# Decode attention over a long cache: key loads a pair ahead, values of the preceding pair inside the next pair's keys

## The chip, the cores and the metric

The kernel runs on one core of a Trainium2 chip. The metric is the device time of one execution in microseconds. Before the change the median of three runs was 1266.62 us (1266.15 to 1267.58). The engines are named as in the profile: PE is TensorE (PEld its weight loads), DVE VectorE, ACT ScalarE, POOL GpSimd, SP SyncE; SP only issues DMAs here.

## The reference

One token is decoded. Its row `x` (448 numbers) gives 16 query heads of 256; each of 8 key/value heads serves two of them. Every head attends to 65536 cached keys and values. A small token MLP of the same row is mixed in by a gate.

```python
q = (x @ wq).reshape(B, Sq, Hq, Dh).transpose(0, 2, 1, 3)
scores = einsum("bhqd,bhkd->bhqk", q, k) * (Dh ** -0.5)     # k, v repeated for the two query heads
p = softmax(scores)
o = einsum("bhqk,bhkd->bhqd", p, v)
a = o.transpose(0, 2, 1, 3).reshape(B, Sq, Hq * Dh) @ wo
h = layernorm(B_x); u = gelu(einsum("bsd,sf->bdf", h, w1) + b1); b = (einsum("bdf,fs->bds", u, w2) + b2)
g = sigmoid((x * gate_w).sum(-1))
return g * a + (1 - g) * b
```

The two caches hold 8 x 65536 x 256 bfloat16 numbers each, 268 MB each, and every number is used once. All else is small.

## The kernel before

*Tiling.* A head's 65536 positions are cut into chunks of 2048 (`CH`): 128 partitions by 16 positions (`NT`). Eight chunks (`BODY`) are a "pair", 16384 positions: 8.39 MB of keys and as many of values. There are four pairs a head (`PPH`), 32 in all (`NP`). A pair's tile is 128 partitions by 128 rows (`NV`) of 256.

*Buffers.* `kring` holds one and a half pairs of keys (192 rows); even pairs lie at rows 0 to 127, odd ones at 64 to 191, and the first four chunks of either parity are taken from the middle 64 rows, so that half a pair's place is free after four chunks. `vbuf` holds one pair of values.

*TensorE, pair by pair.* `keys` (L342 to L353): 16 transposes a chunk (L334, as float32 pairs) bring the keys into PSUM (`kst`); DVE and ACT each copy two of four banks to `ktT` (L616, L751); then 32 small matmuls (`scores`, L353) make the chunk's scores. The transposes of chunk k stand before the scores of chunk k-1. `values` then begins with `maxima` (L374, L376): the pair's largest score is found by DVE, TensorE and DVE in turns (L622 to L645), ACT makes the exponentials `pT` (L738), and DVE rescales the accumulator `acc` (L637, L645). TensorE waits for that (`s_acc`, `sem_exp`), adds the denominators (L392, eight matmuls), and the values (L403, 128 matmuls). The last of them releases `sem_pv`.

*After a head.* DVE takes the sums (`take`, L650), TensorE and DVE turn them (L439, L676), and TensorE multiplies with the head's `A_wo` rows (L450). During the first 14 pairs DVE also works off one part of the MLP (`mixer`, L591 to L609) behind the maxima, and TensorE adds its result (L513).

*SP's order of issues* (L262 to L300). For each pair j: wait until four chunks of pair j-1 are transposed, load K(j); wait until values j-1 are done, load V(j). At a head's start it then waits for the preceding head's projection and loads the next `A_wo` rows. The last two pairs of keys are cut in pieces with semaphores of their own (`sem_kp`, `sem_kq`), the last pair of values in rows 0 to 95, 96 to 111, 112 to 123, 124 to 127. After these come the two pieces of the last `A_wo`.

*The last pair.* Eight matmuls without use (`spin`, L369) stand after its maxima, and before them the MLP's row is added (L386), which DVE made before the last head's loop (`s_mix`, L699 to L702). After 112 rows of values DVE takes the sums while TensorE adds the other 16 rows in the turned form (`late_values`, L424); DVE scales (L663), the last projection runs (L450), and the row goes out (L713, L758, L300).

All loops are run-time loops over registers, one for the heads and one for the pairs within, so the program's code is one pair long.

Of the kernel before, what the change touches and what calls it, by code (L numbers as in the profile page):

```python
# [12 lines left out]
def bass_gated_mix__gqa_block_cached__mixer_token_mlp__decode_kernel(  # L13
# [17 lines left out]
    H = A_k_cache.shape[1]  # L31
# [12 lines left out]
    NT = 16  # L44
# [19 lines left out]
    NFIRST = 96  # L64
    NLATE = 112
    pieces = [(NFIRST, NLATE), (NLATE, 124), (124, NV)]
# [16 lines left out]
    QV = NV // 4  # L83
# [10 lines left out]
    with ctx:  # L94
# [101 lines left out]
        sem_kp = new_sem("sem_kp")  # L196
        sem_kq = [new_sem("sem_kq%d" % i) for i in range(3)]
# [54 lines left out]
        def _(eng):  # L252
# [13 lines left out]
            for j in range(NP):  # L266
                last = j == NP - 1
                if j >= 1:
                    eng.wait_ge(sem_tr[NB - 1], BODY * (j - 1) + DC)
                if j == 0:  # L270
                    load(kring, A_k_cache, j, HV, NV, 0, sem_k)
                    load(kring, A_k_cache, j, 0, HV, 0, sem_kb)
                elif last:
                    for i, sem in enumerate([sem_k] + sem_kq):
                        load(kring, A_k_cache, j, i * QV, (i + 1) * QV, HV, sem)
                elif j == NP - 2:
                    load(kring, A_k_cache, j, HV, NV, 0, sem_k)
                    load(kring, A_k_cache, j, 0, HV, 0, sem_kp)
                else:
                    load(kring, A_k_cache, j, 0, NV, HV * (j % 2), sem_k)  # L280
# [5 lines left out]
                load(vbuf, A_v_cache, j, 0, NFIRST if last else NV, 0, sem_v)  # L286
                if last:
                    for (n0, n1), sem in zip(pieces, sem_vp):
                        load(vbuf, A_v_cache, j, n0, n1, 0, sem)
                g, m = divmod(j, PPH)  # L290
                if m == 0 and 1 <= g < H - 1:
                    eng.wait_ge(s_proj, g)
                    load_wo(g)

            eng.wait_ge(s_proj, H - 1)
# [19 lines left out]
        def _(pe):  # L315
# [3 lines left out]
            def transposes(k, c, j, u16, x2):  # L319
                if k == 0:  # L320
                    pe.wait_ge(sem_k, u16)
                if k == DC:
                    pe.wait_ge(sem_kb, 16)
                    with pe.If(j == NP - 2):
                        pe.wait_ge(sem_kp, 16)
                if k and k % (DC // 2) == 0:
                    with pe.If(j == NP - 1):
                        pe.wait_ge(sem_kq[k // (DC // 2) - 1], 16)
# [17 lines left out]
            def scores(k, c):  # L346
                par = k % 2
                for nt in range(NT):
# [10 lines left out]
            def keys(c0, *where):  # L359
                transposes(0, c0, *where)  # L360
                for k in range(1, BODY):
                    transposes(k, c0 + k, *where)
                    scores(k - 1, c0 + k - 1)
                scores(BODY - 1, c0 + BODY - 1)


            def spin(n):
                for _ in range(n):
                    pe.matmul(kst[:, NB - 1, :], ones_sq[:, :], ktT[:, KTB - 1, 0, 0:512], start=True, stop=True)  # L369
# [9 lines left out]
            def values(j, c0, u16):  # L379
                j1 = pe.snap(j + 1, min_val=1, max_val=NP)  # L380
                maxima(j1)
                with pe.If(j == NP - 1):
# [5 lines left out]
                    spin(8)  # L388
                pe.wait_ge(s_acc, j1)
                pe.wait_ge(sem_exp, j1)  # L390
                for r in range(BODY):
                    pe.matmul(acc[:, DENC:SELC], ones_sq[:, :], pT[:, r, :],  # L392
                              start=False, stop=(r == BODY - 1), skip_group_check=True)

                def some(n0, n1, last=False):
                    if last:
                        piece_wait(n0)
                    else:
                        pe.wait_ge(sem_v, u16)
                    for n in range(n0, n1):  # L400
                        r, nt = divmod(n, NT)
                        o = 32 * (n % 4)
                        ins = pe.matmul(acc[o:o + REP, 0:DH], pT[:, r, 2 * nt:2 * nt + 2], vbuf[:, n, :],  # L403
                                        start=False, stop=False, skip_group_check=True)
                    return ins

                some(0, NFIRST)
                with pe.If(j < NP - 1):
                    some(NFIRST, NV).then_inc(sem_pv, 1)
                with pe.Else():  # L410
                    some(NFIRST, NLATE, last=True).then_inc(s_early, 1)
                    tail()
# [43 lines left out]
            def tail():  # L456
# [3 lines left out]
                spin(1)  # L460
# [39 lines left out]
            x2_reg = pe.alloc_register("x2_reg")  # L500
            pe.reg_mov(x2_reg, 0)
            on = OrderedEngineSet([pe.engine])
            with nc.Fori(0, H, 1, engines=on, head_slot={pe.engine: 0}) as g:
                with nc.Fori(0, PPH, 1, engines=on, head_slot={pe.engine: 0}) as m:
                    j = pe.snap(g * PPH + m, min_val=0, max_val=NP - 1)
                    c0 = pe.snap(j * BODY, min_val=0, max_val=NC)
                    u16 = pe.snap(j * 16 + 16, min_val=16, max_val=16 * NP)
                    keys(c0, j, u16, pe.snap(x2_reg, min_val=0, max_val=NV))
                    values(j, c0, u16)
                    with pe.If(j < FT):  # L510
                        pe.wait_ge(s_pb, j + 1)
                        for q in range(NCG):
                            pe.matmul(prj[32 * q:32 * q + 1, WG:2 * WG], w2cur[:, :],  # L513
                                      gu[:, q * WG:(q + 1) * WG], start=False, stop=True, skip_group_check=True)
                    pe.reg_sub(x2_reg, NV, x2_reg)
                with pe.If(g < H - 1):
                    pe.wait_ge(s_cp, g + 1)
                    clear(acc[:, 0:NACC])
                    by_row(acc[:, SELC:NACC]).then_inc(s_sel, 1)
                    pe.wait_ge(sem_wo, pe.snap(g * 16 + 16, min_val=16, max_val=16 * H))  # L520
                    pe.wait_ge(s_oTn, g + 1)
                    project(range(2 * REP)).then_inc(s_proj, 1)

        @block.vector
        def _(vec):
# [140 lines left out]
            def finish_head(g):  # L666
                take(vec.snap(g * PPH + PPH, min_val=PPH, max_val=NP))
                vec.memset(mrun[:, :], LOW)
                vec.tensor_copy(qcur[:, :, :], qT[:, :, bass.ds(g * REP + REP, REP)])
                vec.drain()  # L670
# [4 lines left out]
                vec.wait_ge(s_sel, g + 1)  # L675
# [5 lines left out]
            vec.tensor_copy(qcur[:, :, :], qT[:, :, 0:REP])  # L681
# [106 lines left out]
```

## Time and profile before

| what | value |
|---|---|
| runs, median (lowest, highest) | 1266.62 us (1266.15, 1267.58) |
| the profiled execution | 1267.84 us, its span 1266.0 us |
| mean clock granted to TensorE | 0.852 |
| busy: PE, PEld, DVE, ACT | 976.4, 889.4, 498.6, 545.5 us |
| read from HBM | 544.22 MB, 430 GB/s over the span |
| chain that ended last, by share | DMA 66%, PE 32%, "issue" 1%, DVE 1% |
| TensorE idle at L334, for keys to land | 144.7 us, 29 times |

The span runs from the first instruction to the last of one profiled execution. "Busy" counts the time in which an engine had an instruction running. The chain is followed back from the last instruction, at each step to what released it. In its rows the three columns are the start, the duration and what ran; "issue" is time in which the engine waited for nothing that the profile shows. In a table of windows each row has the stretch, its length, busy time with the number of instructions for PE, PEld, DVE, ACT and POOL, then the clock granted to TensorE (1.00 is full speed), the share of the DMA engines' time and GB/s.

### The profile page before, as it was taken

To read this page: it belongs to the slowest core of one execution; us is meant where nothing else is said; L and a number is where in the kernel's file an instruction comes from. 1 tells how busy PE (TensorE), PEld (TensorE's weight loads), DVE (VectorE), ACT (ScalarE), POOL (GpSimd) and SP (SyncE) were. 2 spreads that over 40 slices of the span, in tenths; PEclk is the share of its full clock that TensorE was granted. 3 is DMA by queue.
4 is the path that set the end of the run, shared out by engine and by line. 5 is a ranking of instruction groups with operands and counts; after the bars stand their busy time and mean duration, and the time that the engine had idled before them with its cause. 6 is when DMAs were issued, how large, how long until landed. Compare 5 with 4: busy or idle time off the path is not lost.

```text
span 1266.0 us, 39302 instructions
## 1 busy us (share of the span) xinstructions
PE 976.4 (77%) x17210; PEld 889.4 (70%) x17210; DVE 498.6 (39%) x1125; ACT 545.5 (43%) x692; POOL 0.9 (0%) x7
## 2 busy tenths in 40 slices
PE   2877788777787777778687887778877787886888
PEld 2766678766687767677676876668777677776787
DVE  2434345344454444444233433324333334342443
ACT  0544345443355443454334543335443345433554
POOL 0000000000000000000000000000000000000000
PEclk9888788888888878888788898888877788887899
DMA  9999999999999999999999999999999999999998
GB/s 417 430 430 424 431 433 433 433 431 433 433 437 433 433 433 433 437 433 433 431 435 437 431 433 433 433 437 433 429 437 431 435 433 433 435 433 429 431 424 355
DMA packets 12056, 544.39 MB, mean 430 GB/s; under 512 B 1417, under 2 KB 1676, under 8 KB 2956
## 3 DMA queue, kind: packets, MB, share of 16 engines
q1 hardware_dynamic: 11954, 544.22, 99.6%
q8 instruction: 8, 0.13, 0.0%
q14 instruction: 4, 0.03, 0.0%
q10 hardware_dynamic: 90, 0.01, 0.0%
HBM read 544.22 MB, written 0.00 MB: 430 GB/s over the span
## 4 chain that ended last, share of the span: by engine, by line
DMA 66%; PE 32%; issue 1%; DVE 1%; SPq 0%; DVEq 0%
DMA kring<-in_A_k_cache_dram 66%; PE kst L334 25%; PE sps L353 5%; PE acc L403 1%; PE kst L369 0%; PE sps L376 0%; DVE mcol L622 0%; DVE acc L645 0%; PE acc L392 0%; PE sps L374 0%; DVE mrow L627 0%; PE sps L424 0%; DVE mdiag L629 0%; PE sps L431 0%; DVE mcol L625 0%
## 5 line engine op out<-in xcount | busy, mean ns | idle before, releaser
L751 ACT ACTIVATE ktT<-kst 128x1024 bf16<-128x1024 bf16 x512 | 499.7, 1023 | 555.7 <-PE kst L334 555.3
L334 PE MATMUL kst<-ident,kring 128*128 128x128 f32 x4096 | 555.4, 296 | 164.8 <-DMA kring<-in_A_k_cache_dram 144.7
L334 PEld LDWEIGHTS kst<-ident,kring 128*128 128x128 f32 x4096 | 504.5, 154 | 177.5 <-issue 174.6
L616 DVE COPY ktT<-kst 128x1024 bf16<-128x1024 bf16 x512 | 354.1, 692 | 606.9 <-PE kst L334 583.3
L353 PEld LDWEIGHTS sps<-qcur,ktT 128*128 128x128 bf16 x8192 | 237.8, 96 | 5.1 <-issue 2.6
L353 PE MATMUL sps<-qcur,ktT 128*128 128x2 bf16 x8192 | 236.7, 163 | 2.1 <-issue 2.1
L403 PE MATMUL acc<-vbuf,pT 128*2 128x256 bf16 x4080 | 177.2, 356 | 0.0
L403 PEld LDWEIGHTS acc<-vbuf,pT 128*2 128x2 bf16 x4080 | 116.5, 108 | 52.5
L392 PE MATMUL acc<-pT,ones_sq 128*128 128x32 bf16 x256 | 12.7, 190 | 51.0 <-DVE acc L645 51.0
L734 ACT ACTIVATE fade<-mdif 128x2 f32<-128x2 f32 x32 | 6.6, 205 | 95.5 <-DVE mdif L633 95.5
L392 PEld LDWEIGHTS acc<-pT,ones_sq 128*128 128x128 bf16 x256 | 9.5, 106 | 54.1 <-DVE acc L645 53.6
L376 PEld LDWEIGHTS sps<-mdiag,mones 2*128 2x128 f32 x64 | 13.7, 264 | 27.8 <-DVE mdiag L629 27.8
L376 PE MATMUL sps<-mdiag,mones 2*128 2x2 f32 x64 | 16.4, 324 | 21.2 <-DVE mdiag L629 21.2
L622 DVE TENSOR_REDUCE mcol<-sps 128x2 f32<-128x256 f32 x32 | 13.6, 424 | 44.4 <-PE sps L353 44.4
L738 ACT ACTIVATE pT<-sps,mneg 128x64 f32 x128 | 30.5, 336 | 0.0
L755 ACT ACTIVATE z_b<-z_b 128x448 bf16<-128x448 bf16 x14 | 8.1, 579 | 47.9 <-DVE z_b L603 47.9
L374 PE MATMUL sps<-ident,mcol 128*2 128x128 f32 x32 | 9.1, 283 | 24.1 <-DVE mcol L625 24.1
L374 PEld LDWEIGHTS sps<-ident,mcol 128*2 128x2 f32 x32 | 2.6, 80 | 26.9 <-DVE mcol L625 26.9
L645 DVE TENSOR_SCALAR acc<-acc,fader 128x256 f32<-128x256 f32 x32 | 15.8, 492 | 2.5
L650 DVE COPY accs<-acc 128x288 f32<-128x288 f32 x8 | 3.7, 458 | 32.8 <-PE acc L403 32.8
L627 DVE TENSOR_REDUCE mrow<-sps 2x1 f32<-2x128 f32 x32 | 8.9, 278 | 12.0 <-PE sps L374 12.0
L632 DVE TENSOR_SCALAR mneg<-sps 128x2 f32<-128x2 f32 x32 | 5.1, 159 | 19.4 <-PE sps L376 19.4
(108 smaller groups left out, 169.1 us busy)
## 6 DMA issues: line engine op xcount, KB each, us to landing
kring<-in_A_k_cache_dram SPq DMA_DIRECT2D x4, 4096.0 KB, 24.4
kring<-in_A_k_cache_dram SPq DMA_DIRECT2D x4, 2048.0 KB, 26.3
vbuf<-in_A_v_cache_dram SPq DMA_DIRECT2D x1, 6144.0 KB, 27.0
wo_sb<-in_A_wo_dram SPq DMA_DIRECT2D x7, 448.0 KB, 22.8
vbuf<-in_A_wq_dram SPq DMA_DIRECT2D x1, 3072.0 KB, 11.1
vbuf<-in_A_v_cache_dram SPq DMA_DIRECT2D x1, 1024.0 KB, 29.2
vbuf<-in_A_v_cache_dram SPq DMA_DIRECT2D x1, 768.0 KB, 30.6
vbuf<-in_A_wq_dram SPq DMA_DIRECT2D x1, 512.0 KB, 12.7
```

Source lines behind the costliest of these rows:

```text
L334: ins = pe.transpose(kst[:, b, i * P:(i + 1) * P], kring_f[:, at + NT * (k % DC) + 4 * b + i, :], ident[:, :])
L353: ins = pe.matmul(sps[:, 0, 2 * (NT * k + nt):2 * (NT * k + nt) + 2], ktT[:, par, b, ntl * DH + dj:(ntl + 1) * DH:2], qcur[:, dj, :], star ...
L374: pe.transpose(mxT, mcol[:, :], ident[:, :]).then_inc(s_mT, 1)
L376: pe.matmul(mxB, mones[:, :], mdiag[:, :], start=True, stop=True).then_inc(s_mB, 1)
L392: pe.matmul(acc[:, DENC:SELC], ones_sq[:, :], pT[:, r, :], start=False, stop=(r == BODY - 1), skip_group_check=True)
L403: ins = pe.matmul(acc[o:o + REP, 0:DH], pT[:, r, 2 * nt:2 * nt + 2], vbuf[:, n, :], start=False, stop=False, skip_group_check=True)
L616: vec.tensor_copy(ktT[:, k % KTB, b, :], kst_b[:, b, :]).then_inc(sem_ev[b], 1)
L622: vec.tensor_reduce(out=mcol[:, :], in_=scores_all.rearrange("p (n hh) -> p hh n", hh=REP), axis=AX.X, op=ALU.max)
L627: vec.tensor_reduce(out=mrow[:, :], in_=mxT, axis=AX.X, op=ALU.max)
L645: vec.tensor_scalar(acc[:, 0:DENC], acc[:, 0:DENC], fader[:, :], None, op0=ALU.mult).then_inc(s_acc, 1)
L738: ins = act.activation(pT[:, bass.ds(p0, DC), hh:2 * NT:REP], scores_all.rearrange("p (a r n hh) -> p a hh r n", a=2, r=DC, hh=REP)[:, hal ...
L751: act.activation(ktT[:, k % KTB, b, :], kst_b[:, b, :], AF.Copy).then_inc(sem_ev[b], 1)
```

## The change

SP issues the keys a pair further ahead from the third pair on (`LEAD = 2`): after K0, V0, K1, V1 follow K2 and K3 (each in two halves), then V2, K4, V3, K5 and so on, up to K31, V30, and V31 in five pieces. Rows 0 to 47 of V31 go into `kring`, whose lower part no key needs any more; they wait only for pair 30's transposes, the others for values 30.

TensorE has one loop in place of two, with three blocks that are each run or skipped by comparing registers: seven chunks of pair k's keys; the values of pair k-1, and the head's end if that pair was its last; the eighth chunk of pair k, the MLP's part and the maxima. In the first two pairs keys and values take turns as before; from then on each pass runs all three blocks. The scores of a chunk 0 wait for the exponentials of the preceding pair (`sem_exp`), since they overwrite its scores. DVE follows: the head's end stands between the copies of chunks 6 and 7 of the next head's first pair, and the queries of the next head are set with a semaphore of their own (`s_qc`). The matmuls without use are gone. DVE makes the MLP's row after the last maxima.

```diff
-    NFIRST = 96
+    LEAD = 2
     NLATE = 112
-    pieces = [(NFIRST, NLATE), (NLATE, 124), (124, NV)]
+    NRING = 48
+    pieces = [(0, NRING), (NRING, 96), (96, NLATE), (NLATE, 124), (124, NV)]
...
             for j in range(NP):
+                if j == LEAD + 1:
+                    eng.wait_ge(sem_tr[NB - 1], BODY * LEAD)
+                    load(kring, A_k_cache, j, HV, NV, HV, sem_kc[1])
                 if j >= 1:
                     eng.wait_ge(sem_tr[NB - 1], BODY * (j - 1) + DC)
...
+                if j < LEAD:
+                    load_v(j)
+                elif j > LEAD:
+                    load_v(j - 1)
+            for (n0, n1), sem in zip(pieces, sem_vp):
+                if n0 == 0:
+                    eng.wait_ge(sem_tr[NB - 1], BODY * (NP - 1))
+                elif n0 == NRING:
+                    eng.wait_ge(sem_pv, NP - 1)
+                load(kring if n1 <= NRING else vbuf, A_v_cache, NP - 1, n0, n1, 0, sem)
...
-            def scores(k, c):
+            def scores(k, c, j1):
                 par = k % 2
+                if k == 0:
+                    pe.wait_ge(sem_exp, j1)
...
+            def keys(c0, j, *where):
+                j1 = pe.snap(j + 1, min_val=1, max_val=NP)
+                transposes(0, c0, j, *where)
+                for k in range(1, BODY - 1):
+                    transposes(k, c0 + k, j, *where)
+                    scores(k - 1, c0 + k - 1, j1)
+            def last_keys(c0, x2):
+                transposes(BODY - 1, c0 + (BODY - 1), None, None, x2)
+                for k in range(BODY - 2, BODY):
+                    scores(k, c0 + k, None)
...
-                    spin(8)
...
+            with nc.Fori(0, NP + LEAD + 1, 1, engines=on, head_slot={pe.engine: 0}):
+                with pe.If(val(k_reg) < val(cap_reg)):
...
+                    keys(pe.snap(j * BODY, min_val=0, max_val=NC), j,
...
+                with pe.If(val(v_reg) < val(l_reg)):
...
+                    values(v)
...
+                    with pe.If(val(mv_reg) == PPH):
...
+                with pe.If(val(l_reg) < val(k_reg)):
...
+                    last_keys(pe.snap(l * BODY, min_val=0, max_val=NC), pe.snap(x2l_reg, min_val=0, max_val=NV))
...
+                    maxima(pe.snap(l_reg, min_val=1, max_val=NP))
...
-            with nc.Fori(0, H - 1, 1, engines=on) as g:
+            with nc.Fori(0, H, 1, engines=on) as g:
                 with nc.Fori(0, PPH, 1, engines=on) as m:
...
-                    for k in range(BODY):
+                    for k in range(BODY - 1):
                         evacuate(k, c0 + k)
+                    with vec.If(j > 0):
+                        with vec.If(m < 1):
+                            finish_head(g)
+                    evacuate(BODY - 1, c0 + (BODY - 1))
                     maxima(vec.snap(j + 1, min_val=1, max_val=NP), c0)
...
-            take(1, s_early)
+            take(NP, s_early)
```

More of the change, by code (lines that the diff above doesn't have):

```diff
@@ L264, in load, with load_v @@
                               ).then_inc(sem, 16)
[L266 to L280, printed above, removed]
+            load(kring, A_k_cache, 0, HV, NV, 0, sem_k)
+            load(kring, A_k_cache, 0, 0, HV, 0, sem_kb)
+            def load_v(j):
                 if j == 0:
@@ L285, in _ @@
                     eng.wait_ge(sem_pv, j)
[L286 to L289, printed above, removed]
+                load(vbuf, A_v_cache, j, 0, NV, 0, sem_v)
                 g, m = divmod(j, PPH)
@@ L387, in values @@
                                   skip_group_check=True)
[L388 to L409 removed]
+                    piece_wait(0)
+                    some(0, NRING, kring)
+                for n0, n1 in pieces[1:]:
+                    if n0 < NLATE:
+                        last(lambda: piece_wait(n0))
+                        ins = some(n0, n1, vbuf)
+                ins.then_inc(s_early, 1)
+                with pe.If(v < NP):
+                    some(NLATE, NV, vbuf).then_inc(sem_pv, 1)
                 with pe.Else():
[L411 removed]
                     tail()
```

152 lines of the change are left out of this document (98 added, 54 removed).

## The prediction

> **What bounds the kernel now.** I read the head of the page first, for who is busy and whether a transfer is ever missing:
>
> ```profile
> PE 976.4 (77%) x17210; PEld 889.4 (70%) x17210; DVE 498.6 (39%) x1125; ACT 545.5 (43%) x692; POOL 0.9 (0%) x7
> ...
> DMA  9999999999999999999999999999999999999998
> GB/s 417 430 430 424 431 433 433 433 431 433 433 437 433 433 433 433 437 433 433 431 435 437 431 433 433 433 437 433 429 437 431 435 433 433 435 433 429 431 424 355
> ...
> q1 hardware_dynamic: 11954, 544.22, 99.6%
> ```
>
> The DMA engines are full in every slice but the last, at one rate. Then the chain that ended last, in order of time, around the last pairs:
>
> ```profile
> 1097.88 27.32 DMA kring<-in_A_k_cache_dram
> 1125.33 5.38 PE kst L334 x32
> ...
> 1135.90 28.93 DMA kring<-in_A_k_cache_dram
> 1164.95 6.14 PE kst L334 x32
> ...
> 1185.49 1.86 PE kst L334 x16
> 1187.35 1.59 PE sps L353 x64
> 1188.97 0.42 DVE mcol L622
> ...
> 1192.84 0.40 PE acc L392 x8
> 1193.24 5.59 PE acc L403 x111
> 1198.82 0.41 issue
> ...
> 1224.86 5.14 PE acc L403 x127
> ...
> 1254.49 2.68 PE kst L369 x8
> 1257.38 3.86 PE acc L403 x101
> 1261.27 0.47 DVE accs L650
> ...
> 1262.41 0.80 PE sps L424 x32
> 1263.47 0.40 PE prj L450 x16
> ```
>
> Up to 1164.95 each pair begins when its keys land. Landings (the first L334 of a pair) are 38.70 us apart, 39.83 where an A_wo load lies between: 618.81, 657.52; 1125.33, 1164.95. A pair is 16.78 MB, so 433.5 GB/s, and one K or V load is 19.35 us of the stream. From pair 29's landing I continue the stream: before, K30 1203.65, V30 1223.0, K31 1242.35, V31 1261.7; the V31 pieces (issue from 1230.06 on, 27.0 to 30.7 us to land) come to 1257.06 up to 1262.05, and the last A_wo to about 1263. That fits a stream with no gap to within 0.4 us. TensorE ends 1261.24, beside it. So both stream and TensorE end the kernel, and all the time there is to win is what lies after 1262; a transfer issued too late is lost one for one.
>
> **The change part by part.** The profiled execution took 1267.84 us for a span of 1266.0 (1.84 around it); the median of the runs is 1266.62, so I add span differences to that median.
>
> *Bytes, rate.* The same 544.22 MB on the same queue, in another order: K(j+1) goes ahead of V(j). Cost 0, while every load is issued before the load ahead of it has drained. So I check each issue, with a step beginning at K(s)'s landing T. Four chunks of keys take 10.4 us (1125.33 to 1135.90), so K(s+1) is issued at T+10.5; V(s-1) drains until T+19.35: 8.8 us to spare. Seven chunks take 20.5 in pair 29 (1164.95 to 1185.49), of which 6.14 are the first two; these vary from 5.04 to 6.67 in the chain, so about 20.1. Values then start at T+20.2, after V(s-1) landed, take 5.6 to 6.0 (L392 0.40, L403 5.14 to 5.59), and V(s) is issued at T+26.3, with K(s+1) draining until T+38.7: 12 us to spare. Last chunk 3.45 (1185.49 to 1188.94) and maxima 2.3 end the step at T+32.5, 6 us before the next keys. A head's end adds 3.6 (652.7 to 655.9 and its gap) in a step of 39.83. The mixer (4.4 us on DVE, pairs 0 to 13) now runs ahead of the next pair's first evacuation and not beside the values: T+33 to T+38. All hidden; cover gone costs at most what exceeds 6 us, then 8.8.
>
> *What stood idle per pair.* TensorE's waits for the maxima (51.0 + 24.1 + 21.2 us at L392, L374, L376, 3 us a pair): the exponentials now have a whole seven chunks of cover. It gains nothing in a steady pair, where TensorE waits for keys anyway (144.7 us).
>
> *The two split loads at pairs 2 and 3.* K3's second half waits for all of pair 1 (about 95) and drains from 112 on; K3's first half waits for half of pair 2, which starts after values 1, about 107.3 + 9.1 = 116.4, and the queue has work until 121.9: 4 us to spare. V2 is queued right behind it on SP. Cost 0.
>
> *The last step, by the clock of before.* K31 now lands 19.35 earlier, at 1223.0; V30 at 1242.35. Then in TensorE's order, each from a row above:
> - seven chunks 0.1 + 20.1: 1243.2, 0.9 after V30, so the keys decide;
> - branches and registers 0.4 (the "issue" row), denominators 0.4, 128 values 5.2: 1249.2. The rest of V31 is issued here. V31's first 48 chunks (now into the free half of the key ring) land at 1249.6, so the queue is all but empty. The shortest whole DMA in the trace, the x row, takes 1.36 from issue to landing (0.73 to 2.09): chunks 48 to 95 land by 1249.25 + 1.36 + 7.26 = 1257.9 and not 1256.9. The gap is 1.0 us; V31's end 1262.7 to 1263.0, A_wo's 1264;
> - gap 0.4, last chunk 3.45: 1253.05;
> - maxima to denominators 3.90 (1188.94 to 1192.84): 1256.95;
> - denominators 0.4; meanwhile DVE prepares the MLP row (L699, L701, L702: 0.28 + 0.16 + 0.24, with drains 0.75), which it did ahead of the last head and now does after the last maxima; four small matmuls 0.25: 1257.8. So 0.45 is new on the path;
> - 112 values: 1262.5 (below);
> - from the last of these to the end 1261.24 to 1266.0, 4.76 in the same steps: 1267.3. V31's last piece is wanted at 1263.7 and A_wo at 1264.7, so the stream's gap is covered by 0.7 us.
>
> *The eight spin matmuls gone.* They ran inside the maxima (1254.49, 2.68 us) and kept the clock up. The windows by stretch show what the clock is worth:
>
> ```profile
> 1193.00:1199.00 6.00, 5.82 (x136) 3.82 (x133) 0.00 (x0) 0.00 (x0) 0.00 (x0) 0.64 1.01 437
> ...
> 1224.80:1230.00 5.20, 5.20 (x131) 3.49 (x128) 0.00 (x0) 0.00 (x0) 0.00 (x0) 0.69 1.02 435
> ...
> 1257.30:1261.20 3.90, 3.90 (x116) 2.72 (x112) 0.00 (x0) 0.00 (x0) 0.00 (x0) 0.82 0.93 361
> ```
>
> 128 values took 5.59 at 0.64 granted and 5.14 at 0.69; 112 took 3.86 at 0.82: duration times clock is 3.6 for 128, 3.15 for 112. Without the spin I take 0.67 for values 31, the middle of the two pairs without one: 4.7, against 3.9. The lowest grant in the trace, 0.50 (1165 to 1170, after a wait for keys), would make it 6.3, 1.6 more. [...]
>
> *Sum.* 1267.3 against 1266.0: +1.3 us, and 1266.62 + 1.3 = 1267.9. Its own profiled execution would be about 1269.1.
>
> Bounds. Lower: first two chunks 5.04 (-0.6), both groups of values at the clock of the spun ones (-0.8, -0.8) give -0.9, but A_wo at 1263 and L450 to the end, 2.53, hold it at -0.5. Upper: first chunks 6.67 (+1.0), values at 0.64 (+0.4, +0.2) or at 0.50 (+1.6), and up to six more branches on this path than before, at 0.31 to 0.42 each where the sequencer is not ahead (+2.1): +5 to +6.
>
> **Rivals.** A measurement of this kernel can tell about 0.2%, 2.5 us, from no change.
>
> 1. *The last step is longer than I add up* (slower). The place is the stretch from K31's landing to the end, which TensorE now walks alone; it decides once 1.2 us more than my sum come together from the clock (0.50 to 0.82 in the rows) and the branches. For it: the chain there has no slack left after V30, and every row of it varies by 10%. Against: TensorE's queue runs ahead of most branches, seen in values with a branch at 96 and no gap. Price: +2.6 to +6, 1269.2 to 1272.
>
> 2. *Fetching code in the first passes holds V1 up* (slower). Before, the first pass stood still with nothing to wait for 5.41 us (24.07 to 29.48), 1.78 (before the last scores) and 2.46 (before L513), later passes not; the page counts 8 instruction packets of 0.13 MB. Now the first passes jump over blocks not yet run: past the values, back, past the keys. V1 was issued at 65.42 and the stream runs dry at about 72.1 (K1's landing 73.5, less 1.4), so 6.7 to spare. Three jumps at the mean 3.2 less the 1.78 replaced: 7.9, a gap of 1.2; at 5.41 each 14.4, a gap of 7.8. Against: the fetch ahead may have loaded the blocks. Price on top of the sum: 1269.1 to 1275.7. [...]
>
> 3. *The code no longer stays loaded.* TensorE's program is some 5% longer, all inside one loop. If a pass fetched three pages at 3.2, 9.6 us against 6 free would cost 3.6 in each of 30 steps: about 1375. Nothing in the trace points at a limit just there.
>
> 4. *Faster.* The stream would have to end 2.5 us sooner; landings 38.70 or 39.83 apart all the way from pair 2 to pair 29 leave no gap to close, and the tail after A_wo gives 0.5. 1264 or less needs something the trace does not show.
>
> That the loads are not really ahead would show as an unchanged order of landings and give 1266.6, within "no change".
>
> **How the numbers follow.** No change that can be told, with 1267.9 as its time (its own range 1265.5 to 1269.1): 0.55. Rival 1: 0.22. Rival 2: 0.13. Rival 3: 0.05. Faster: 0.05. Slower is 0.22 + 0.13 + 0.05 = 0.40. The range of 1265.5 to 1272.0 leaves out rival 3, most of faster, and the upper half of rival 2, together 0.16.
>
> **What would show it.** Landings of keys still 38.70 apart; TensorE's waits at L392, L374, L376 unchanged for the maxima (they still run alone) but the one for the exponentials gone; K31's transposes at about 1223 and values 30 ending about 1249; the last group of 112 values at about 1258 and taking 4.5 to 5; the stream's DMA share low for about 1 us near 1250. I am wrong if key landings drift apart in the middle, if V1 is issued after 72, or if the last V piece, and not TensorE, is what ends the chain.

## The result: slower by half a per cent

| | before | after |
|---|---|---|
| runs, median (lowest, highest) | 1266.58 us (1266.07, 1267.58) | 1273.26 us (1272.60, 1274.62) |
| the profiled execution, its span | 1267.84, 1266.0 us | 1273.45, 1271.7 us |
| clock granted to TensorE | 0.852 | 0.840 |

The ratio is 1.0053, with a 95% interval of 1.0040 to 1.0066. That is slower by 6.7 us where 1.3 us was forecast, and above the range given.

The head of the page after the change, with the same rows as those shown of before:

```profile
PE 941.5 (74%) x17201; PEld 884.7 (70%) x17201; DVE 498.2 (39%) x1125; ACT 545.8 (43%) x692; POOL 0.9 (0%) x7
...
DMA  9999899999999999999999999999999999999998
GB/s 415 430 399 428 377 429 429 443 429 429 429 429 443 429 429 451 439 410 449 441 429 429 443 429 429 429 443 429 429 429 429 443 429 429 429 451 439 429 429 344
...
q1 hardware_dynamic: 11810, 544.22, 99.2%
q8 instruction: 9, 0.15, 0.0%
```

The bytes are the same. One digit of the DMA row has changed from 9 to 8: the fifth slice (127 to 159 us), at 377 GB/s where before had 431. The third slice (64 to 95 us) has 399 where before had 430. A slice is 31.8 us, so these rows say that the stream broke off early in the run, once above all.

The chain, in order of time, for the last step:

```profile
1200.58 27.11 DMA kring<-in_A_k_cache_dram
...
1227.82 5.88 PE kst L344 x32
...
1248.38 3.59 PE acc L400 x128
1251.97 0.69 issue
1252.66 1.96 PE kst L344 x16
1254.62 1.59 PE sps L365 x64
...
1261.06 5.82 PE acc L400 x112
```

K31's transposes begin at 1227.82 where 1223.1 was forecast: 4.7 us late. From there to the end of the span it takes 43.9 us; the forecast had 44.2, and before, which ended at 1266.0, would have had 42.9 from 1223.1. So 4.7 us came from late keys and 1.0 from the last step: 5.7, the difference of the two spans. The medians differ by 6.7, because the profiled execution of before, 1267.84 us, took longer than each of its six timed runs, while that of after lies near its median.

*Where the keys became late.* In the same view a key load lands where its DMA row ends. Each pair's keys should land 19.35 us, one load of the stream, earlier than before. Pair 6's landed at 268.12 before, so the forecast for them is 248.77; after had them at 253.95, 5.2 late. From there to K31's landing at 1227.69 the distance is 973.74 us, and in the forecast 1222.88 - 248.77 = 974.11 (1222.88 is the forecast's 1223.0, counted to the end of the DMA row and not to the first transpose). In between the landings stand 38.70 or 39.83 apart as before (566.02, 604.72, 643.43, 682.13, 721.96). All that K31 is late by was lost in the first 254 us, and only 0.4 us of it came back.

The windows by stretch show the loss. First before, then after, the same three stretches (columns as in the prediction, the last three being granted clock, DMA share, GB/s):

```profile
70.00:75.00 5.00, 1.38 (x7) 1.39 (x8) 0.17 (x1) 0.00 (x0) 0.00 (x0) 0.50 1.14 488
...
150.00:155.00 5.00, 4.00 (x19) 4.01 (x20) 1.38 (x2) 1.32 (x2) 0.00 (x0) 0.50 0.97 419
155.00:160.00 5.00, 5.00 (x77) 4.98 (x76) 2.65 (x4) 3.62 (x5) 0.00 (x0) 0.88 0.97 419
```

```profile
70.00:75.00 5.00, 0.91 (x14) 0.41 (x7) 0.00 (x0) 0.00 (x0) 0.00 (x0) 0.50 0.94 357
...
150.00:155.00 5.00, 4.54 (x51) 4.40 (x51) 1.38 (x2) 2.29 (x3) 0.00 (x0) 0.63 0.63 210
155.00:160.00 5.00, 5.00 (x97) 4.98 (x95) 2.77 (x4) 3.38 (x4) 0.00 (x0) 1.00 0.57 249
```

Between 150 and 160 us the difference is 5 x (419 - 210) + 5 x (419 - 249) = 1895 GB/s x us, which is 4.4 us at 433.5 GB/s. Between 70 and 75 it is 1.5, of which a third comes back at once. Summed over all windows of 5 us up to a point, after is 1.0 to 2.3 us behind from 75 to 150, and 6.5 behind at 160; this sum, which goes by bytes, stands at 7.2 at 280 and at 5.3 at 300, near the 5.2 by which the landings are late.

Why it broke off shows in SP's own timeline of after, its DMA issues (V1, K2 and K3 in halves together, V2, K4):

```profile
70.64 0.33 SPq L264 DMA_DIRECT2D vbuf<-in_A_v_cache_dram  x1
85.49 33.48 SPq L264 DMA_DIRECT2D kring<-in_A_k_cache_dram  x4
119.02 0.43 SPq L264 DMA_DIRECT2D vbuf<-in_A_v_cache_dram  x1
153.57 0.33 SPq L264 DMA_DIRECT2D kring<-in_A_k_cache_dram  x1
```

and in TensorE's timeline around K4's issue (idle time before a group, and what ended it, in brackets):

```profile
134.65 3.67 PE L344 MATMUL kst<-ident,kring 128*128 128x128 f32 x16 [0.68 <-issue]
141.17 3.67 PE L344 MATMUL kst<-ident,kring 128*128 128x128 f32 x16 [2.85 <-DVE ktT L674]
...
145.53 3.65 PE L344 MATMUL kst<-ident,kring 128*128 128x128 f32 x16
```

K4 waits for four chunks of pair 3. These took from 134.65 to 153.5, 18.9 us, where the forecast had 10.5. The second chunk waits 2.85 us for a DVE copy, and every chunk up to the fourth takes 3.65 us or more for its 16 transposes, not 1.95: in windows of 1 us the granted clock is 0.50 from 134 to 153. DVE's timeline says what it did meanwhile:

```profile
135.74 0.34 DVE L649 TENSOR_SCALAR wtmp<-hbT,params 128x448 bf16<-128x448 bf16 x1 [0.18 <-issue]
...
139.71 0.39 DVE L667 TENSOR_TENSOR gu<-wtmp,z_b 128x448 bf16<-128x448 bf16 x1
140.42 1.29 DVE L674 COPY ktT<-kst 128x1024 bf16<-128x1024 bf16 x2 [0.32 <-issue]
```

That is pair 2's part of the MLP, 135.7 to 140.1, behind the maxima of pair 2 and ahead of the first copies of pair 3's keys. When K4 was issued the queue was empty; a finer window has not one byte between 149.80 and 153.50 (V2's landing itself is put at 152.1):

```profile
149.80:153.50 3.70, 3.70 (x30) 3.64 (x27) 1.38 (x2) 1.47 (x2) 0.00 (x0) 0.50 0.00 0
```

*The first passes.* TensorE's timeline has three long waits for nothing that the profile shows, each where code is reached that has not run yet or a pass begins anew: ahead of pair 0's last chunk, which is reached by a jump over the values; within values 0, after 80 of its matmuls, where kernel.py has no branch (its branches stand after rows 48, 96 and 112); and ahead of pair 1's keys, after the jump back (these had landed at 72.46, so they account for less than half of the last wait):

```profile
51.43 3.54 PE L344 MATMUL kst<-ident,kring 128*128 128x128 f32 x16 [8.06 <-issue]
...
68.09 2.52 PE L400 MATMUL acc<-vbuf,pT 128*2 128x256 bf16 x48 [2.90 <-issue]
74.70 5.59 PE L344 MATMUL kst<-ident,kring 128*128 128x128 f32 x32 [4.09 <-issue]
```

V1 is issued at 70.64 (before 65.42).

### The profile page after: what moved, and what is told of

Same layout as the page of the kernel before. It is cut to its first block, busy times and chain, and to the rows that moved or that the text cites. A ratio compares the mean times of both kernels' runs of the same rounds, so it can differ in the third digit from the quotient of the medians.

```text
span 1271.7 us, 40084 instructions
## 1 busy us (share of the span) xinstructions
PE 941.5 (74%) x17201; PEld 884.7 (70%) x17201; DVE 498.2 (39%) x1125; ACT 545.8 (43%) x692; POOL 0.9 (0%) x7
## 4 chain that ended last, share of the span: by engine, by line
DMA 61%; PE 35%; DVE 2%; issue 2%; DVEq 0%; ACT 0%; SPq 0%
DMA kring<-in_A_k_cache_dram 61%; PE kst L344 27%; PE sps L365 6%; PE acc L400 2%; PE sps L388 0%; DVE mcol L680 0%; ACT z_b L816 0%; PE acc L458 0%; PE sps L386 0%; PE acc L393 0%; DVE ktT L674 0%; DVE mrow L685 0%; DVE z_b L655 0%; DVE wtmp L653 0%; DVE z_b L659 0%
## 5 line engine op out<-in xcount | busy, mean ns | idle before, releaser
L344 PE MATMUL kst<-ident,kring 128*128 128x128 f32 x4096 | 574.9, 303 | 251.6 <-DMA kring<-in_A_k_cache_dram 198.0
L344 PEld LDWEIGHTS kst<-ident,kring 128*128 128x128 f32 x4096 | 522.2, 158 | 266.6 <-issue 259.7
L400 PE MATMUL acc<-vbuf,pT 128*2 128x256 bf16 x4032 | 121.6, 281 | 2.9 <-issue 2.9
L400 PEld LDWEIGHTS acc<-vbuf,pT 128*2 128x2 bf16 x4032 | 94.2, 86 | 21.9 <-issue 3.4
L393 PEld LDWEIGHTS acc<-pT,ones_sq 128*128 128x128 bf16 x256 | 8.6, 97 | 12.4 <-issue 7.0
```

Source lines behind the costliest of these rows:

```text
L344: ins = pe.transpose(kst[:, b, i * P:(i + 1) * P], kring_f[:, at + NT * (k % DC) + 4 * b + i, :], ident[:, :])
L393: pe.matmul(acc[:, DENC:SELC], ones_sq[:, :], pT[:, r, :], start=False, stop=(r == BODY - 1), skip_group_check=True)
```

## The experiments

Three theories. *M*: pair 2's part of the MLP holds pair 3's first copy, so K4 is issued after the stream ran dry; priced at 3 to 4 us. *Code*: fetches of code in the first passes hold V1, K2 and K3 up; 1 to 2 us. *Last step*: the step from K31 on is longer by about 1 us, in part because the MLP's row is made on the path. The rival to all three: the new order of loads by itself costs the stream something.

### Moving the MLP's parts

The parts run in pairs 3 to 16, that is, none between pair 2 and pair 3; the same shift on ACT and TensorE, with the counts of their semaphores raised by `J0` at the start:

```diff
+    J0 = 3
...
-                    with vec.If(j < FT):
-                        mixer(j)
+                    with vec.If(j < J0 + FT):
+                        with vec.If(j > J0 - 1):
+                            mixer(j)
```

> The changed kernel with the MLP's parts in pairs 3 to 16 in place of 0 to 13, so that none stands behind the maxima of pair 2. Theory M (the MLP part of pair 2 holds the copies of pair 3's first chunk, K4 is issued at 153.6 where V2 lands at 152.1, and the stream loses about 4 us): the second chunk of keys 3 starts near 137.5 in place of 141.2, K4 is issued by about 149, the moved bytes at 160 us fall no more than 2 to 3 us behind the kernel before (6.5 in the changed kernel), and the time is 3.5 to 4 us below the changed kernel, about 1269.4. Rival H (keys 2 and keys 3 back to back are too slow by themselves, at a granted clock of 0.50): K4 still after 152, less than 1 us gained, 1272.5 or more.

Measured 1269.47 us, ratio 1.0018 (1.0009 to 1.0027). SP's and TensorE's timelines of this run:

```profile
69.68 0.33 SPq L265 DMA_DIRECT2D vbuf<-in_A_v_cache_dram  x1
...
119.34 0.43 SPq L265 DMA_DIRECT2D vbuf<-in_A_v_cache_dram  x1
146.48 0.33 SPq L265 DMA_DIRECT2D kring<-in_A_k_cache_dram  x1
```

```profile
135.01 6.26 PE L345 MATMUL kst<-ident,kring 128*128 128x128 f32 x32 [0.72 <-issue]
...
141.92 1.95 PE L345 MATMUL kst<-ident,kring 128*128 128x128 f32 x16
```

and its windows:

```profile
150.00:155.00 5.00, 5.00 (x96) 4.98 (x93) 2.70 (x4) 3.70 (x5) 0.00 (x0) 1.00 1.00 433
155.00:160.00 5.00, 4.51 (x159) 3.62 (x155) 0.07 (x1) 0.93 (x2) 0.00 (x0) 1.00 1.01 433
```

V2 is issued at the same time as in after (119.34 against 119.02), and K4 7.1 us sooner: the wait of 2.85 is gone, and the clock, which is 0.50 at 135 here too, is back at 1.00 from 141 and not from 154. The stream is full where it was empty. K31's transposes begin at 1224.22, 3.6 sooner; the time falls by 3.8 us, of the 6.7. M is shown. The order of loads is unchanged in this run, and from pair 6's keys (250.92) to K31's (1224.09) it took no longer than forecast, 973.17 us, which leaves little for the rival.

The control is the kernel before with its MLP in pairs 8 to 21:

> The kernel before with the MLP's parts in pairs 8 to 21. Theory M holds only where nothing stands between the maxima and the next keys; here the values do, which need no copies. So no change: within 0.1% of 1266.6. If the MLP's place cost time here too, 1 to 4 us less.

1265.92 us, ratio 0.9998 (0.9989 to 1.0008): in the old order moving the MLP is worth nothing. V1 was issued at 65.84.

### Another order of the blocks

The last chunk, the MLP's result and the maxima come first in a pass, then the seven chunks, then the values, so that the first pass doesn't jump over the values to the last chunk:

```diff
             with nc.Fori(0, NP + LEAD + 1, 1, engines=on, head_slot={pe.engine: 0}):
+                with pe.If(val(l_reg) < val(k_reg)):
+                    ...
                 with pe.If(val(k_reg) < val(cap_reg)):
...
-                with pe.If(val(l_reg) < val(k_reg)):
-                    ...
```

> The changed kernel with the three blocks of TensorE's loop in the order last chunk, keys, values in place of keys, values, last chunk; the order of the work is the same in every pair, only the jumps of the first passes differ. Theory C (the first passes jump over code that is not loaded, V1 is issued at 70.6 and not at 65.4, and the stream loses 1.5 to 2 us there): the 8.06 us gap before pair 0's last chunk goes or shrinks to some 3 us, V1 is issued by 66, and the time falls by 1.5 to 2 us to about 1271.5. Rival (the loss near 70 to 95 us is of the stream, not of V1's issue): V1 earlier, time within 0.7 us of the changed kernel's 1273.3.

> Both edits, with the MLP's parts in pairs 8 to 21, when the pairs are steady. If the two gaps are all that delays the stream, keys 31 land at 1222.8 to 1223.5 (1227.8 in the changed kernel), the last step keeps its 43.9 us, and the time is that of the kernel before plus 0.5 to 1.5: 1267 to 1268. If something else delays it (the new order of loads itself), 1270 or more with keys 31 after 1226.

The first gave 1271.13 us (1.0034, 1.0021 to 1.0046), the second, with the MLP in pairs 8 to 21 as well, 1269.19 (1.0016, 1.0007 to 1.0025). As a cure for V1 both missed. TensorE's timeline of the first still waits ahead of pair 0's last chunk, and longer than in after:

```profile
56.58 3.67 PE L344 MATMUL kst<-ident,kring 128*128 128x128 f32 x16 [9.36 <-issue]
```

V1 was issued at 71.50 and 75.23. What a late V1 costs can be read across the runs: in the sum over windows of 5 us the stream is behind the kernel before at 80 us by 0.0 us where V1 went out at 65.84 (the control), 0.8 at 69.68, 1.0 at 70.64, 3.2 at 71.50 and 5.6 at 75.23. The second kernel shows M a second time: K4 at 146.54 against 151.40.

### The last step

On top of that second order: 64 rows of V31 into the key ring, not 48, and DVE makes the MLP's row in pair 28, not after the last maxima.

```diff
-    NRING = 48
+    NRING = 64
...
                     maxima(vec.snap(j + 1, min_val=1, max_val=NP), c0)
+                    with vec.If(g > H - 2):
+                        with vec.If(m < 1):
+                            vec.wait_ge(s_proj, H - 1)
+                            ...
+                            vec.tensor_scalar(brow, brow1, bcast[:, 2:3], None, op0=ALU.add).then_inc(s_mix, 1)
```

> The same with two edits for the last step: rows 0 to 63 of V31 in the key ring in place of 0 to 47, so that less is left to load after values 30, and the MLP's row made in pair 28 in place of after the last maxima. If the last pieces of V31 end the kernel (a gap of 1.1 us before them, values 31 taking 5.9 us for waits), 1.0 to 1.5 us less than the kernel without them and 1266 to 1266.8, the same as the kernel before. If TensorE's chain ends it, only the MLP row's 0.4.

1270.96 us (1.0031, 1.0020 to 1.0041), no gain over 1269.19. The profile separates two things. From the first maximum on DVE to the values of V31 it takes 4.34 us in this run's chain, and 4.82 or 4.83 in the chains of after, of the kernel without this edit and of six others: the row on the path costs 0.5 us. The 16 rows more gave nothing that can be seen, the values of V31 taking 5.59 and 5.63. The whole last step is 42.9 us here and 44.0 without the edit, but the rest of that difference is in K31's first 32 transposes (5.32 against 5.88), which vary in every run (a kernel below without this edit also has 42.7). K31 itself came 2.7 later, with waits of 1.64 within values 0 and 2.74 ahead of keys 1 where there had been 1.62, and the instruction queue has 10 packets, not 7. The row's price is shown; in this profiled execution more than that was lost again in the first passes.

### V1 in two pieces

If only V1's issue matters, its first 48 rows can be loaded as soon as values 0 have used theirs (with the MLP in pairs 8 to 21):

```diff
+                    if j == 1:
+                        eng.wait_ge(s_first, 1)
+                        load(vbuf, A_v_cache, j, 0, NRING, 0, sem_v1)
                     eng.wait_ge(sem_pv, j)
-                load(vbuf, A_v_cache, j, 0, NV, 0, sem_v)
+                load(vbuf, A_v_cache, j, NRING if j == 1 else 0, NV, 0, sem_v)
```

> The changed kernel with the MLP's parts in pairs 8 to 21 and V1 loaded in two pieces: rows 0 to 47 as soon as TensorE has used these rows of V0 (about 63), the others after all of values 0 (about 70 to 75, as before). TensorE's code and its gaps in the first passes stay. Theory C (V1's late issue is what the stream loses there): the moved bytes stay within 0.7 us of the kernel before from 70 to 200 us, keys 31 land at 1222.8 to 1223.8, the last step takes 43.9, and the time is that of the kernel before plus 0.7 to 1.5, about 1267.6, with little spread between runs. Rival (the stream loses there by itself, by the order or by code being fetched beside it): still 1269 or more.

> The same with the two edits for the last step (rows 0 to 63 of V31 in the key ring, the MLP's row made in pair 28). The last step took 42.9 us with them, from the first transposes of keys 31 to the end, against 43.9 to 44.2 without. So with keys 31 at 1223: 1265.9 for the span and 1266.2 to 1267.0 for the time, the same as the kernel before. It is faster than that only if something but the stream ends the kernel.

1270.91 us (1.0036, 1.0023 to 1.0050) and, with the last step's edit, 1278.74 (1.0096, 1.0083 to 1.0109). V1's first piece went out at 63.99, and the stream was only 1.1 us behind at 75; but it was 1.7 behind at 120 and 5.5 at 130. TensorE's timeline of the first:

```profile
51.57 3.67 PE L350 MATMUL kst<-ident,kring 128*128 128x128 f32 x16 [7.65 <-issue]
...
70.17 2.87 PE L406 MATMUL acc<-vbuf,pT 128*2 128x256 bf16 x49 [4.52 <-issue]
78.02 6.16 PE L350 MATMUL kst<-ident,kring 128*128 128x128 f32 x32 [4.99 <-issue]
```

Keys 1 begin at 78.02 (after: 74.70), so K2 and K3's first half go out later, and V2 at 123.44. The idea was too narrow: what a wait of TensorE holds up is all that TensorE releases, one load after another. In the second kernel the waits are 6.94, 1.21, 6.53 and 9.63 with 11 instruction packets, keys 1 begin at 86.49 and K31's transposes at 1233.98: longer waits and later keys go together. From its maxima to the values of V31 it again took 4.33.

### Is it the distance that is jumped?

256 matmuls that are never run, inside the block that the first pass jumps over:

```diff
+                    with pe.If(val(v_reg) > NP):
+                        some(0, 64, vbuf)
+                        some(64, 128, vbuf)
+                        some(0, 64, vbuf)
+                        some(64, 128, vbuf)
```

> The changed kernel with 256 more matmuls in the block of values that are never run (the branch ahead of them is always taken). If code is fetched where a jump lands (theory C), the first passes stand still longer, V1 is issued later than 70.6, and 2 us or more are added. If TensorE's whole loop must stay loaded (the prediction's rival 3) and 512 instructions more pass a limit, gaps with nothing to wait for appear in every pass, the instruction packets go from 9 to several hundred, and the time is far above 1300. If code has no part in it, 1273 as it was.

1273.44 us (1.0053), the same as after; the waits are 7.95, 3.03 and 3.81 and the packets 9. A miss: with 256 matmuls more to skip the first wait was no longer (7.95 us against 8.06), and the count of packets shows no fetch of the code that is never reached (9, 0.15 MB, as in after).

### Fetching the blocks ahead of their use

One empty pass ahead of pair 0's keys, which jumps over all three blocks:

```diff
-            cap_reg = reg("cap_reg", 1)
+            cap_reg = reg("cap_reg", 0)
...
-            with nc.Fori(0, NP + LEAD + 1, 1, engines=on, head_slot={pe.engine: 0}):
+            with nc.Fori(0, NP + LEAD + 2, 1, engines=on, head_slot={pe.engine: 0}):
...
+                with pe.If(val(cap_reg) < 1):
+                    pe.reg_mov(cap_reg, 1)
```

> The changed kernel with one more pass of TensorE's loop ahead of all others that skips all three blocks, while the first keys are still on their way (TensorE idle from 19.4 to 23.9). It jumps once to the end of each block. Theory C' (a jump costs a fetch of the code where it lands, once, whatever the distance; it delays everything TensorE releases, V1 and K2 and K3's first half alike): the gaps with nothing to wait for of 8.06, 2.90 and 4.09 us shrink to a third, keys 0 start a few us later, near 29 as in the kernel before, V1 is issued by 67 and keys 1 start when they land, near 73.6. The gap at K4 by the MLP part of pair 2 stays, so the time falls by 1 to 2 us to about 1271.7. If the gaps are no fetches of code or come back on entering the blocks: 1273 as it was.

> The same with the MLP's parts in pairs 8 to 21. Theories C' and M together: the stream keeps up with the kernel before, within 0.7 us from 70 us on, keys 31 land at 1222.8 to 1223.8, the last step takes 43.9 us, and the time is that of the kernel before plus 0.7 to 1.5, about 1267.5. If there is a third cause, 1269 or more.

> The same with rows 0 to 63 of V31 in the key ring and the MLP's row made in pair 28, with which the last step took 42.9 us twice. If keys 31 land at 1223.3: 1266.2 for the span, the kernel before's time within 0.1%.

1279.24 us (1.0093, 1.0074 to 1.0112); with the MLP in pairs 8 to 21 1275.30 (1.0065, 1.0048 to 1.0081); with the last step's edit too 1282.59 (1.0116, 1.0099 to 1.0134). TensorE's timeline of the second:

```profile
39.90 6.49 PE L345 MATMUL kst<-ident,kring 128*128 128x128 f32 x32 [21.15 <-issue]
...
61.00 1.96 PE L345 MATMUL kst<-ident,kring 128*128 128x128 f32 x16 [0.57 <-issue]
...
75.42 1.95 PE L401 MATMUL acc<-vbuf,pT 128*2 128x256 bf16 x48 [2.23 <-issue]
81.06 6.39 PE L345 MATMUL kst<-ident,kring 128*128 128x128 f32 x32 [3.68 <-issue]
```

The empty pass does nothing but jump, and TensorE stood idle for 21.15 us (20.24 and 27.39 in the other two), where in after it waited 5.13 for keys 0. After it the wait of 8.06 ahead of pair 0's last chunk is 0.57: where that jump has been made once, the second time costs next to nothing. The other two waits stayed, 2.23 within values 0 and 3.68 ahead of keys 1 (3.03 and 3.10 in the first kernel). Code that was only jumped over had not been run yet, which would explain the first of them; what these two wait for no run here shows. And the price was only moved, and grew: keys 0 begin at 39.90 and not at 23.86, V1 goes out at 77.41, and the stream was 8.5 us behind at 100.

The same, with the empty pass made from 2.7 us on, while TensorE waits for the first transfers anyway. TensorE's query matmuls, which have to stand behind it, were put at the end of the loop, in a block that runs once:

```diff
-            pe.wait_ge(sem_misc, 16 * 5)
-            ...
-            clear(prj[:, 0:2 * WG])
...
                 with pe.If(val(cap_reg) < 1):
                     pe.reg_mov(cap_reg, 1)
+                    pe.wait_ge(sem_misc, 16 * 5)
+                    ...
+                    clear(prj[:, 0:2 * WG])
```

> The changed kernel with the MLP's parts in pairs 8 to 21, and with a pass that skips all three blocks, as before keys 0 in the kernel dry8, but now at about 2.5 us, while TensorE waits for the first transfers anyway; the matmuls that make the queries stand behind it, at the end of the loop, run once. The empty pass took 20.2 us there (keys 0 started at 38.5 and not at 23.9). Theory C' (jumps into code not yet loaded cost some 5 us each and hold up what TensorE releases): the empty pass ends near 22, the queries near 27, keys 0 start at 28 to 31, V1 is issued at 66 to 69 with its threshold at 72, keys 1 start when they land near 73.6, the moved bytes stay within 1 us of the kernel before, keys 31 land at 1223 to 1224, and the time is 1267 to 1268. Rival (the new order of loads itself makes the stream slower in the first 150 us): 1269 or more though V1 is issued in time.

> The same with rows 0 to 63 of V31 in the key ring and the MLP's row made in pair 28. With the first passes cured, 42.9 us from keys 31 to the end, 1266 to 1266.8: the same as the kernel before. If its other place of the code costs fetches again (keys 0 started at 47.8 in its sister with the late empty pass), V1 is issued after 72 and the time is 1269 or more.

> The early empty pass alone, the MLP's parts left in pairs 0 to 13. The gap at K4 by the MLP part of pair 2 remains: K4 issued at 152 to 153 against V2's landing near 151, 3.5 to 5 us lost there, 1271 to 1272.5. Together with the kernel that moves the MLP's parts alone (1269.5) and the one with both, this shows how far the two causes add up.

1890.67 us (1.4934), 1929.95 (1.5249) and, with the MLP in pairs 0 to 13, 1894.74 (1.4957). The head of the first one's page:

```profile
DMA  9966785667856678666786667866678666786653
...
q8 instruction: 290, 4.75, 1.2%
...
PE 54%; issue 40%; DVE 3%; DMA 2%; DVEq 0%; ACTq 0%; ACT 0%
```

and TensorE's timeline in one step of the middle:

```profile
1020.20 3.77 PE L401 MATMUL acc<-vbuf,pT 128*2 128x256 bf16 x75 [1.49 <-issue]
1027.57 2.73 PE L401 MATMUL acc<-vbuf,pT 128*2 128x256 bf16 x48 [3.59 <-issue]
1033.72 3.56 PE L345 MATMUL kst<-ident,kring 128*128 128x128 f32 x16 [3.42 <-issue]
...
1056.46 1.75 PE L345 MATMUL kst<-ident,kring 128*128 128x128 f32 x7 [15.33 <-issue]
```

None of the three expectations has this; it is the mechanism of the prediction's rival 3. There are 290 instruction packets instead of 9, about 8 for each of 36 passes, 16.4 KB each. The loop now reaches over nearly all of TensorE's program, and the code no longer stays loaded: by these counts every pass fetches the loop again, and issue is 40% of the chain. These three runs say nothing on the first passes; they show that this loop does not stay loaded, where that of after does, with its 9 packets.

### What the runs come to

| kernel | V1 issued | K4 issued | K31's first transpose | to the end | median |
|---|---|---|---|---|---|
| after | 70.64 | 153.57 | 1227.82 | 43.9 | 1273.26 |
| MLP from pair 3 | 69.68 | 146.48 | 1224.22 | 44.2 | 1269.47 |
| other order | 71.50 | 151.40 | 1225.77 | 43.7 | 1271.13 |
| other order, MLP from pair 8 | 75.23 | 146.54 | 1226.87 | 44.0 | 1269.19 |
| the same, last step's edit | 75.66 | 150.10 | 1229.54 | 42.9 | 1270.96 |
| empty pass, MLP from pair 8 | 77.41 | 154.38 | 1230.49 | 42.7 | 1275.30 |

K31's first transpose and the rest are from one profiled execution of each, the median from all its runs; the execution of the fourth row took 1272.75 us, the longest of its eleven. With M cured, what is left of after's 6.7 us is 2.9 (1269.47 against 1266.59 on the same chip). The spans of the profiled executions differ by 2.4 (1268.4 against 1266.0), 1.1 of it on K31's keys (1224.22 against 1223.1) and 1.3 on the last step (44.2 against 42.9). No version here beats the kernel before, and its landings 38.70 us apart leave nothing in the stream to win. A version free of the waits in the first passes was not reached, so that their share is 1 to 2 us follows from the windows and is not shown by a run that took them away.

## Why the prediction was wrong

*"Bytes, rate ... Cost 0, while every load is issued before the load ahead of it has drained."* The condition was right, and it is where the change lost most of its time. The failed step is the check of it: it was made for a step "beginning at K(s)'s landing T", thus for steady pairs only. In those it held: the landings stayed 38.70 and 39.83 us apart from 254 us on. The step that begins with keys already in place, pair 3's, was not checked. There T was 134.65, and no byte moved from 149.8 until K4 was issued. Four chunks at the forecast's 10.5 would have put K4 at 145.2, 4.6 us ahead of that and 6.9 ahead of V2's landing, not 8.8. They took 18.9.

*"The mixer ... now runs ahead of the next pair's first evacuation ... All hidden; cover gone costs at most what exceeds 6 us."* The place was right and 4.4 us its length. The cover named was the wait for the next keys, and in pair 3 there is none, since K3 was there. "All hidden" and its 6 us of cover are what failed. And the price was more than the wait: 2.85 us of waiting went with 7.4 us of delay (18.9 against 11.5 with the MLP moved), since TensorE then worked at half clock (0.50) until 153.5, and with the MLP moved only until about 140. A bound of "at most what exceeds" 6 us counted a delay only once.

*"The two split loads at pairs 2 and 3 ... 4 us to spare. Cost 0."* K3's first half and V2 were issued in time for the queue, at about 119; that step held, although everything was 2 us later than in the forecast (116.4). It stopped one load too early: K4 comes after V2, and was the one that failed.

*Rival 2, code in the first passes*, had 13%. Its mechanism is shown for the first wait: 8.06 us, and 0.57 where the jump had been made once before; for the waits of 2.90 and 4.09 it is argued from their place (1.85 of the last went on keys 1). The forecast's mean was 3.2 each. Of the 9 instruction packets of after, each about 1 us long, two begin within the first wait (43.4 and 48.3 us) and one at each of the others (65.6 and 70.4); four more moved while TensorE worked on (26.7, 36.4, 55.5 and 77.3). V1 went out at 70.64, short of the 72.1 from which the rival was to decide; the stream's loss up to 150 us, 1 to 2 us, is at the low end of the gaps that it was priced at, 1.2 to 7.8. What the rival missed is that K2 and K3 wait behind the same places. After the first passes nothing of it is seen: in after the loop jumps in every pass, the whole run has 9 instruction packets, and from 254 us on TensorE's longest wait for nothing that the profile shows is 0.7 us.

*Rival 3, the code no longer stays loaded*, had 5% and was wrong here, 9 packets against 8. It isn't far off: the kernel with the query matmuls in its loop is that case, at 1890.67 us. The forecast of 3.6 us a step was much too mild for it: the step shown lost 23.8 us to four waits. The three pages a pass at 3.2 us each that it was summed from were an assumption that no run shows; here it is about 8 packets of 16.4 KB a pass. Between the loop of after and this one no run varies the length, so at which length that begins is not shown.

*The last step* was summed to 44.2 us and took 43.9, so rival 1 did not decide; but the sum is right by luck, through errors that cancel. The seven chunks took 20.05 (20.1). Values 30 were mis-sized: 5.2 in the forecast, 3.59 measured, for the clock was 1.00 there; 3.6 us is the product of duration and clock that the prediction had found. The maxima took 3.77 (3.90), the way from there to the values of V31 1.07 (0.85), the tail 4.8 (4.76). Values 31 took 5.82 and not 4.7, and it was the clock and no missing piece: TensorE was busy almost throughout, in these windows of after:

```profile
1260.90:1263.50 2.60, 2.60 (x52) 1.62 (x52) 0.00 (x0) 0.00 (x0) 0.00 (x0) 0.50 0.99 420
1263.50:1265.00 1.50, 1.50 (x36) 0.96 (x28) 0.00 (x0) 0.00 (x0) 0.00 (x0) 0.50 1.01 421
1265.00:1266.90 1.90, 1.85 (x41) 1.05 (x32) 0.00 (x0) 0.00 (x0) 0.00 (x0) 0.62 0.99 379
```

I had taken 0.67, the middle of two rows; the clock granted here, 0.50 until 1265.0 and then 0.62, is nearer to the 0.50 that the forecast had only in its upper bound. The MLP's row on the path was forecast at 0.45 and cost 0.5 (4.82 against 4.33).

*The waits for the maxima* behaved as forecast: the one for the exponentials, at the denominators, fell from 51.0 to 9.8 us, TensorE's idle time for keys grew from 144.7 to 198.0, and it bought nothing.

The list of what would show the prediction wrong had "if key landings drift apart in the middle" and "if V1 is issued after 72". Neither happened, nor did the third sign, a last V piece that ends the chain. The list named V1 and the middle, and the loss was in between.

## What to carry to other kernels

When a stream is the bound, check each issue against the load ahead of it at the hand-over from the start-up to the steady loop with its own times, since the work that waiting for data hides in a steady step has no cover there. Count a short wait of TensorE with the half clock that may go on after it (here 0.50 for 12.4 us behind a wait of 2.85). And a loop put together from blocks under conditions can stand still in its first passes, here for up to 8.06 us at a time; see that the loads which keep the stream fed don't hang on those places, and keep once-only code out of the loop, which here cost 617 us.

## What the runs showed of the hardware that I had not expected

- In after the granted clock was 0.50 ahead of a wait of 2.85 us and stayed so for 12.4 us behind it (141.1 to 153.5), though TensorE was busy for 12.33 of them; 16 transposes took 3.65 us against 1.95. With the MLP moved, and so without the wait, the clock was back at 1.00 some 6 us after keys 3 began (135.01 to 141).
- In the first passes TensorE stood still for 2.90, 4.09 and 8.06 us in after, up to 9.63 in other versions, and an empty pass of jumps took 20 to 27 us. The distance had no part in the longest: 256 matmuls more under its jump changed nothing (8.06 to 7.95).
- A loop that stays loaded cost 9 instruction packets in the whole run, and one with the query matmuls inside it 290, and 617 us (1890.67 against 1273.26). The other loops, without them, have 7 to 11 packets; none lies in between.
